# First decoder layer's groups 0 to 5 read as one stream of 64 KiB rows, V's sum kept apart from V, more of the weighting on VectorE

## The chip, the cores and the metric

One NeuronCore of a Trainium2 chip runs the whole kernel. The time is device microseconds of one execution, the median of several runs. VectorE, ScalarE, TensorE and GpSimd are written DVE, ACT, PE and POOL in the profile; SP issues every transfer from device memory.

## What is computed

Two layers of attention, each followed by a small MLP, for one token:

```python
x = x + _A_ref(_layernorm(x), K, V, wq, wo)   # 32 heads, 4096 cached positions, 128 per head
x = x + _B_ref(_layernorm(x), w1, b1, w2, b2) # 512 -> 1376 -> 512, gelu
x = x + _A_ref(_layernorm(x), K, V, wq, wo)   # the same caches and weights again
x = x + _B_ref(_layernorm(x), w1, b1, w2, b2)

def _A_ref(x, k, v, wq, wo):
    q = heads(x @ wq)
    p = softmax(q . k * 128 ** -0.5)          # over the 4096 positions
    return merge(p . v) @ wo
```

Everything is float32. The caches are 64 MiB each and are read once in each layer, so the work is mostly the reading: about 285 MB in all.

## The kernel before

**Groups and chunks.** The 32 heads are taken in 8 groups of 4. K of a group is a block of 128 partitions x 16384 floats (64 KiB on each partition, 8 MiB in all), cut into 8 chunks c = 0 to 7 of 2048 floats (1 MiB); V of a group has the same size and the same cut. A group's slice of `wq`, and of `wo`, is as large as one chunk. The first layer takes the groups in order 0 to 7, the second in the order 7 to 0 and starts on what is still in SBUF. Nearly all of SBUF is one tile, `arena`: three blocks of 8 chunks, then a place for the first `wq` (at `HELD`), and a place of two chunks (`PAIR`) for the weights of a group.

**Order of the transfers.** All are issued by SP through `load` (L87), in program order, and land in that order. In the first layer a group n takes three of them: K (L507, in block (2n+1) mod 3), V (L552, in block (2n+2) mod 3), and one of two chunks with this group's `wo` and the next group's `wq` (L582, in `PAIR`). A transfer is issued when what lay in its place has been read for the last time. SP's queue is in order: a waiting issue holds those behind it.

**A group of the first layer, n = 0 to 5.**
1. `scores` (L232): PE multiplies the query by the 8 chunks of K, into the PSUM bank `pS`.
2. `softmax` (L235 to L255): on DVE the maximum (L236) and small steps, on ACT the exponential (L244), on PE four transposes (L246), on DVE the copy of the weights to `pt` (L248) and the reciprocal of their sum.
3. The weighting of V by `pt`: DVE multiplies chunks 0 to 3, one at a time (`weighted`, L274, 128x2048), ACT chunks 4 to 7 in 16 pieces each (`weighted_by_act`, L269).
4. The sum of the 8 chunks, in the place of chunk 0, on DVE: three adds of two chunks at once (`add_pair`, L279, 128x4096), one of chunk 0 and 1 (L589, 128x2048), one fold to half the length (L287).
5. Between them the next query: `queries` weights `wq` on DVE (L213, L215), PE sums over the partitions (L217), DVE takes the diagonal (L221, L223). Only then can `scores` of the next group begin.
6. The rest is late: inside the next group's `scores`, after chunk 4, PE sums the folded V over the partitions (L292); DVE scales it (L297 to L300) and weights `wo` (L326, L328), which ends the use of `PAIR`; PE adds that to the output row (L332). DVE runs these ahead of the next `softmax`.

DVE's and PE's instructions are pinned in the order of the program (`pin`). Group 6 has PE multiply V by the weights (`values`, L262) in place of steps 3 and 4. Group 7 ends the layer: K in two halves, V in parts, then its `wo`, and after it come `w1`, `w2` and the first of the second layer's K.

Of the kernel before, what the change touches and what calls it, by code (L numbers as in the profile page):

```python
# [55 lines left out]
VAR_AT = 1  # L56
PAIRS = (0, 2, 4, 6), ((4, 6, 0, 2), (2, 0, 4, 6))


@with_exitstack  # L60
def decode_layers(ctx: ExitStack, tc: tile.TileContext, k, v, w, w1, w2, out):
    nc = tc.nc
# [30 lines left out]
    def chunk(t, i=0):  # L93
        return t[:, NC * i : NC * (i + 1)].rearrange("p (j n) -> p j n", j=4)
# [58 lines left out]
    mx, mb = small("mx", 32), small("mb", 32)  # L153
    for t in (zq, mx, mb):
        nc.vector.memset(t, 0.0)

# [78 lines left out]
    def softmax(sc, nsc, p, hold):  # L235
        top = nc.vector.tensor_reduce(mx[:, 0:1], pS, axis=AX.X, op=ALU.max)  # L236
# [11 lines left out]
        nc.vector.tensor_copy(pt, pT[:, :, :, :C].rearrange("p b j c -> p j c b"))  # L248
# [22 lines left out]
    def weighted(pt, t, c):  # L271
        own = t.rearrange("p b (j d) -> p b j d", j=J)
        weight = pt[:, :, c, :].rearrange("p j b -> p b j")[:, :, :, None].to_broadcast([P, 4, J, DH])
        nc.vector.tensor_tensor(own, own, weight, op=ALU.mult)  # L274

# [180 lines left out]
    for layer in range(2):  # L456
# [23 lines left out]
        for n, g in enumerate(order):  # L480
            first, final = n == 0, n == G - 1
            pairs = None
            if layer == 0 and n < G - 2:
                pairs = PAIRS[0]
            if layer == 1 and 1 < n < G - 2:
                pairs = PAIRS[1][n % 2]

# [3 lines left out]

            if layer == 1 and n == 0:
                tiles = [(c, here["k", g, c]) for c in range(C)]
# [14 lines left out]
            for c, t in tiles:  # L508
                scores(z, c, t)
                if late is not None and c == 4:  # L510
                    late[0]()
# [18 lines left out]
            elif layer == 1 and n == 1:  # L530
# [27 lines left out]
            if pairs:  # L558
# [4 lines left out]
                for c in pairs[:2]:  # L563
                    for i in (0, 1):
                        weighted(pt, here["v", g, c + i], c + i)
                add_pair(v_home, *pairs[:2])
# [138 lines left out]
```

## Time and profile before

| | |
|---|---|
| time, median of 3 runs | 673.04 us (672.83 to 673.28) |
| the profiled execution | 672.88 us, of which the span 671.0 us, 1.88 us around it |
| mean granted clock of PE | 0.725 of full speed |
| PE, DVE, ACT busy | 46%, 63%, 32% of the span |
| time that the packets of SP's queue took | 99.2% of the span of 16 DMA engines |
| read from device memory | 284.92 MB, 425 GB/s over the span |

Busy shares are means over stages that differ. For each engine a timeline gives start, duration, line and shapes of its instructions, with the idle time before them and what ended it in square brackets. "Clock" is the share of full speed that PE was granted in a stretch.

### The profile page before, as it was taken

Reading aid. Unit: us, or ns where it says so; the run is one execution under the profiler, and the core shown is the slowest. Engines: PE = TensorE matmul, PEld = TensorE weight load, DVE = VectorE, ACT = ScalarE, POOL = GpSimd, SP = SyncE. Lnnn points to the kernel's source line nnn. Section 1 sums busy time; section 2 is a strip of 40 time slices with the busy share of each in tenths; the row PEclk is TensorE's granted clock in tenths of the full one; section 3 lists DMA queues with packets and bytes.
Section 4 is the critical chain, followed back from the end, with each engine's and each line's share of the span. In section 5 each row is a group of like instructions: output and inputs, shape, how many; then the busy total and the mean of one; then the engine's idle time right before and its main releaser. Section 6 shows DMA issues by size and latency. Waiting matters only on the chain.

```text
span 671.0 us, 5941 instructions
## 1 busy us (share of the span) xinstructions
PE 307.4 (46%) x2196; PEld 83.0 (12%) x2196; DVE 424.0 (63%) x520; ACT 215.3 (32%) x697; POOL 5.2 (1%) x26
## 2 busy tenths in 40 slices
PE   1401603406117054166788985604416126065597
PEld 1100100101001011011124311101101001011124
DVE  3059779598797886972322414289697795983513
ACT  0047064190560823802011200083290650910010
POOL 1000000000000000000000000000000000000000
PEclk9965855857658557577699999755757558567799
DMA  9999999999999999999999999999999999999997
GB/s 377 438 438 438 435 438 438 403 461 438 438 430 404 434 438 426 430 435 425 430 416 403 414 438 439 427 430 438 427 438 438 426 434 405 452 438 417 428 414 300
DMA packets 11548, 285.36 MB, mean 425 GB/s; under 512 B 1280, under 2 KB 1408, under 8 KB 3840
## 3 DMA queue, kind: packets, MB, share of 16 engines
q1 hardware_dynamic: 11520, 284.99, 99.2%
q8 instruction: 17, 0.28, 0.2%
q14 instruction: 11, 0.09, 0.0%
HBM read 284.92 MB, written 0.07 MB: 425 GB/s over the span
## 4 chain that ended last, share of the span: by engine, by line
DMA 65%; PE 20%; DVE 11%; another core or an unknown queue 1%; issue 1%; SPq 1%; ACT 0%; DVEq 0%
DMA arena<-in_k 41%; DMA arena<-in_w 13%; DMA arena<-in_v 12%; PE pS L232 11%; DVE arena L328 4%; PE pO L292 3%; PE pO L262 2%; DVE arena L274 1%; DVE arena L215 1%; DVE arena L297 1%; DVE smalls L299 1%; DVE arena L326 1%; PE pO L430 1%; DVE arena L279 1%
## 5 line engine op out<-in xcount | busy, mean ns | idle before, releaser
L269 ACT ACTIVATE arena<-arena,pt 128x128 f32<-128x128 f32 x640 | 188.0, 386 | 42.7 <-DMA arena<-in_v 38.5
L232 PE MATMUL pS<-arena,smalls 128*8 128x512 f32 x1024 | 142.4, 708 | 78.5 <-DMA arena<-in_k 74.3
L279 DVE TENSOR_TENSOR arena<-arena 128x4096 f32<-128x4096 f32 x30 | 132.6, 4420 | 0.3
L217 PE MATMUL pS<-arena,smalls 128*128 128x512 f32 x20 | 20.8, 1141 | 195.0 <-DVE arena L215 195.0
L244 ACT ACTIVATE arena<-pS,smalls 128x512 f32<-128x512 f32 x16 | 12.4, 777 | 300.9 <-DVE smalls L243 300.9
L274 DVE TENSOR_TENSOR arena<-arena,pt 128x2048 f32<-128x2048 f32 x40 | 89.0, 2286 | 29.0 <-DMA arena<-in_v 26.1
L232 PEld LDWEIGHTS pS<-arena,smalls 128*8 128x8 f32 x1024 | 28.5, 100 | 195.5 <-issue 174.6
L236 DVE TENSOR_REDUCE smalls<-pS 128x1 f32<-128x512 f32 x16 | 11.0, 687 | 61.4 <-PE pS L232 61.4
L262 PE MATMUL pO<-arena,pt 128*4 128x512 f32 x368 | 44.8, 632 | 8.7 <-DMA arena<-in_v 7.9
L304 DVE STREAM_TRANSPOSE arena<-pO 128x512 f32<-128x512 f32 x6 | 4.3, 717 | 57.1 <-PE pO L262 57.1
L215 DVE SCALAR_TENSOR_TENSOR arena<-arena,smalls 128x512 f32<-128x512 f32 x45 | 33.8, 752 | 1.6
L328 DVE SCALAR_TENSOR_TENSOR arena<-arena,smalls 128x512 f32<-128x512 f32 x39 | 29.3, 752 | 1.4
L332 PE MATMUL pB<-arena,smalls 128*1 128x512 f32 x26 | 14.4, 637 | 33.3 <-DVE arena L328 33.3
L217 PEld LDWEIGHTS pS<-arena,smalls 128*128 128x128 f32 x20 | 5.0, 310 | 198.2 <-DVE arena L215 198.2
L297 DVE TENSOR_TENSOR arena<-pO,ident 128x512 f32<-128x512 f32 x10 | 6.9, 692 | 31.3 <-PE pO L292 31.3
L246 PE MATMUL pO<-ident,arena 128*128 128x128 f32 x64 | 13.2, 341 | 25.6 <-ACT arena L244 25.2
L589 DVE TENSOR_TENSOR arena<-arena 128x2048 f32<-128x2048 f32 x10 | 22.9, 2291 | 0.3
L292 PE MATMUL pO<-arena,smalls 128*128 128x512 f32 x40 | 19.8, 618 | 0.0
L399 ACT ACTIVATE smalls<-smalls 128x4 f32<-128x4 f32 (+1 forms) x6 | 1.2, 206 | 43.6 <-DVE smalls L392 25.4
L250 DVE STREAM_TRANSPOSE smalls<-smalls 128x32 f32<-128x32 f32 x16 | 3.4, 212 | 17.4 <-ACT arena L244 17.4
L262 PEld LDWEIGHTS pO<-arena,pt 128*4 128x4 f32 x368 | 9.2, 89 | 41.1 <-issue 35.9
L246 PEld LDWEIGHTS pO<-ident,arena 128*128 128x128 f32 x64 | 8.5, 169 | 39.5 <-ACT arena L244 34.1
(119 smaller groups left out, 211.9 us busy)
## 6 DMA issues: line engine op xcount, KB each, us to landing
arena<-in_w SPq DMA_DIRECT2D x13, 2048.0 KB, 11.5
arena<-in_k SPq DMA_DIRECT2D x5, 4096.0 KB, 21.1
arena<-in_v SPq DMA_DIRECT2D x2, 4096.0 KB, 31.6
arena<-in_w SPq DMA_DIRECT2D x6, 1024.0 KB, 30.9
arena<-in_k SPq DMA_DIRECT2D x1, 6144.0 KB, 19.9
arena<-in_v SPq DMA_DIRECT2D x2, 2048.0 KB, 36.1
arena<-in_w SPq DMA_DIRECT2D x7, 512.0 KB, 11.4
arena<-in_v SPq DMA_DIRECT2D x3, 1024.0 KB, 44.7
```

The lines of the kernel that those rows point to most:

```text
L215: pin(nc.vector.scalar_tensor_tensor(t, wt[:, c, :], xc[:, c : c + 1], t, op0=ALU.mult, op1=ALU.add))
L217: pin(nc.tensor.matmul(at, one.to_broadcast([P, P]), t, start=True, stop=True))
L232: pin(nc.tensor.matmul(pS[32 * j : 32 * j + C, :], z[:, j, C - 1 - c : 2 * C - 1 - c], kt[:, j, :], start=(c == 0), stop=(c == C - 1)))
L246: nc.tensor.transpose(pT[:, b].rearrange("p j r -> p (j r)"), p[:, P * b : P * (b + 1)], ident)
L262: nc.tensor.matmul(pO[32 * j : 32 * j + 4, :], pt[:, j, c, :], by_head(vt)[:, j], start=(i == 0), stop=(i == of - 1))
L269: nc.scalar.activation(own, own, AF.Copy, scale=pt[:, j, c, b : b + 1])
L274: nc.vector.tensor_tensor(own, own, weight, op=ALU.mult)
L279: pin(nc.vector.tensor_tensor(a, a, b, op=ALU.add))
L292: pin(nc.tensor.matmul(pO, one.to_broadcast([P, P]), total[:, b, :], start=b == 0, stop=b == n - 1))
L328: pin(nc.vector.scalar_tensor_tensor(t, wt[:, d, :], on[:, d : d + 1], t, op0=ALU.mult, op1=ALU.add))
L332: pin(nc.tensor.matmul(pB[0:1, :], one, t, start=n == 0, stop=n == G - 2))
L589: pin(nc.vector.tensor_tensor(total, total, other, op=ALU.add))
```

## The change

**The stream.** K, V, `wo` and `wq` of groups 0 to 5, and K of group 6, become units of one chunk in the order of use: k0 (8 units), v0 (8), wq1, k1 (8), wo0, v1 (8), wq2, k2 (8), wo1 and so on. The host cuts this list into rows: row 0 has 4 units, rows 1 to 14 have 8 each (64 KiB on each partition). Each row is one transfer into block (r+2) mod 3. Row r is issued when all units of row r-3 are used up (`flow`, `done`), so a row now holds parts of K, V and weights, and waits for the last use of any of them. What the prediction speaks of: row 6 is v2; row 8 is k3 chunk 7, wo2 and v3 chunks 0 to 5; row 9 takes row 6's place, row 11 takes row 8's.

**V's sum.** It gets a place of its own behind the three blocks (`total`), no longer that of V's chunk 0.

**The weighting.** `weighted_two` multiplies two neighbouring chunks at once (128x4096). A table gives each group the chunks that ACT weights and the order of the steps on DVE: `W` two chunks multiplied, `w` one, `a24` chunks 4, 5 added to 2, 3, `s01` the first two into the sum, `t2` one more into the sum, `q` the next query's weighting, `r` its diagonal. `LATE` says after which chunk of the next `scores` the late sum is put. ACT weights 12 of 48 chunks, before 24; DVE weights 36.

**Softmax, both layers.** The reciprocal is taken of the 32-wide broadcast, in place of a copy and a reciprocal of one column; one instruction fewer. In the second layer the pairs that DVE weights are also taken two at once.

The core of the diff (all of the table but two lines, and the host's packing, left out):

```diff
+PLANS = (
...
+    ((5, 6, 7), "W01 W23 a02 w4 a04 a06 q s01 r"),
+    ((2, 3, 6), "W01 W45 s01 a24 w7 t2 q t3 r t6 t7"),
...
+LATE = 6, 6, 4, 4, 6, 6
...
-        lt, l, lr, rl = small("mt", 32), small("l"), small("lr", 32), small("rl")
+        lt, l, lr = small("mt", 32), small("l"), small("lr", 32)
         nc.vector.transpose(lt, mx)
         nc.vector.tensor_reduce(l, lt[:, :C], axis=AX.X, op=ALU.add)
-        nc.vector.tensor_copy(lt, l.to_broadcast([P, 32]))
+        nc.vector.reciprocal(lt, l.to_broadcast([P, 32]))
         nc.vector.transpose(lr, lt)
-        nc.vector.reciprocal(rl, lr[:, 0:1])
-        return pt, rl
+        return pt, lr[:, 0:1]
...
+    def weighted_two(pt, t, c):
+        own = t.rearrange("p (b j d) -> p b j d", j=J, d=DH)
+        weight = pt[:, :, c : c + 2, :].rearrange("p j c b -> p (c b) j")[:, :, :, None].to_broadcast([P, 8, J, DH])
+        return nc.vector.tensor_tensor(own, own, weight, op=ALU.mult)
...
+    def early_values(n, pt, xc):
+
+        by_act, plan = PLANS[n]
+        total = chunk(arena[:, 3 * BLOCK : 3 * BLOCK + NC])
+        for c in by_act:
+            weighted_by_act(pt, here["v", n, c], c)
+        steps = plan.split()
...
+        a, b = steps.index("q"), steps.index("r")
+        for s in steps[:a]:
+            step(s)
+        z = queries(n + 1, xc, here["wq", n + 1, 0], pS, short=True,
+                    between=lambda: [step(s) for s in steps[a + 1 : b]])
+        done(("wq", n + 1, 0))
+        for s in steps[b + 1 :]:
+            step(s)
+        return z, total, folded(total)
...
+    def flow():
+
+        while len(loaded) < len(ROWS) and (len(loaded) < 3 or used.issuperset(ROWS[len(loaded) - 3])):
+            r = len(loaded)
+            loaded.append(load((r + 2) % 3 * BLOCK, rows_of[r][:, : NC * len(ROWS[r])]))
...
+    def done(*units):
+        used.update(units)
+        flow()
...
             for c, t in tiles:
                 scores(z, c, t)
-                if late is not None and c == 4:
+                if layer == 0 and n <= EARLY:
+                    done(("k", n, c))
+                if late is not None and c == (4 if layer else LATE[n - 1]):
                     late[0]()
...
+            elif early:
+                z, total, n_left = early_values(n, pt, xc_l)
+
+                def late_sum(rl=rl, ot=ot, n=n, total=total, n_left=n_left):
+                    sum_of_folded(total, n_left)
+                    summed_wo(scaled_out_of_folded(rl, ot), here["wo", n, 0], ot[:, :U])
+                    done(("wo", n, 0))
```

**SP at the start of the program, before:** `in_w` brings the weights, `in_k` and `in_v` the caches; a size is partitions x floats.

```order
L87 DMA arena<-in_w 128x2112
L87 DMA arena<-in_k 128x16384
L87 DMA arena<-in_v 128x16384
L87 DMA arena<-in_w 128x4096
L87 DMA arena<-in_k 128x16384
L87 DMA arena<-in_v 128x16384
```

The same place now, `in_rows` being the new array:

```order
L105 DMA arena<-in_w 128x2112
L105 DMA arena<-in_rows 128x8192
L105 DMA arena<-in_rows 128x16384 x14
L105 DMA arena<-in_v 128x16384
L105 DMA arena<-in_w 128x4096
```

Nineteen transfers (seven of K, six of V, six of weights) became fifteen; after them comes V of group 6 as before.

**DVE in group 2, from the weighting of V to the fold, before** (`arena<-arena,pt` is a multiplication by the weights, `arena<-arena` an addition, `pS` the next query's sum):

```order
L274 TENSOR_TENSOR arena<-arena,pt 128x2048 x4
L279 TENSOR_TENSOR arena<-arena 128x4096
L213 TENSOR_SCALAR arena<-arena,smalls 128x512
L215 SCALAR_TENSOR_TENSOR arena<-arena,smalls 128x512 x3
L279 TENSOR_TENSOR arena<-arena 128x4096
L221 TENSOR_TENSOR arena<-pS,ident 128x512
L223 TENSOR_REDUCE smalls<-arena 128x4
L279 TENSOR_TENSOR arena<-arena 128x4096
L589 TENSOR_TENSOR arena<-arena 128x2048
L287 TENSOR_TENSOR arena<-arena 128x1024
```

The same stretch of group 2 now:

```order
L296 TENSOR_TENSOR arena<-arena,pt 128x4096 x2
L322 TENSOR_TENSOR arena<-arena 128x4096
L291 TENSOR_TENSOR arena<-arena,pt 128x2048
L322 TENSOR_TENSOR arena<-arena 128x4096 x2
L231 TENSOR_SCALAR arena<-arena,smalls 128x512
L233 SCALAR_TENSOR_TENSOR arena<-arena,smalls 128x512 x3
L327 TENSOR_TENSOR arena<-arena 128x2048
L239 TENSOR_TENSOR arena<-pS,ident 128x512
L241 TENSOR_REDUCE smalls<-arena 128x4
L351 TENSOR_TENSOR arena<-arena 128x1024
```

One more chunk is multiplied, and the next query's steps (L231 to L241) moved from the middle of the additions to their end.

**DVE in group 3 now** (before, group 3 had the same rows as group 2):

```order
L296 TENSOR_TENSOR arena<-arena,pt 128x4096 x2
L327 TENSOR_TENSOR arena<-arena 128x2048
L322 TENSOR_TENSOR arena<-arena 128x4096
L291 TENSOR_TENSOR arena<-arena,pt 128x2048
L327 TENSOR_TENSOR arena<-arena 128x2048
L231 TENSOR_SCALAR arena<-arena,smalls 128x512
L233 SCALAR_TENSOR_TENSOR arena<-arena,smalls 128x512 x3
L327 TENSOR_TENSOR arena<-arena 128x2048
L239 TENSOR_TENSOR arena<-pS,ident 128x512
L241 TENSOR_REDUCE smalls<-arena 128x4
L327 TENSOR_TENSOR arena<-arena 128x2048 x2
L351 TENSOR_TENSOR arena<-arena 128x1024
```

Five chunks are weighted on DVE where it was four, single additions take the place of double ones, and the third L327 (step `t3`), which row 11 waits for, stands behind the next query's weighting (L231, L233).

More of the change, by code (lines that the diff above doesn't have):

```diff
@@ L153, in decode_layers @@
     mx, mb = small("mx", 32), small("mb", 32)
-    for t in (zq, mx, mb):
-        nc.vector.memset(t, 0.0)
+    for t, start in ((zq, 0.0), (mx, 1.0), (mb, 0.0)):
+        nc.vector.memset(t, start)
     def of_32(t, n, i=0):
@@ L273, in weighted, with two, step @@
         weight = pt[:, :, c, :].rearrange("p j b -> p b j")[:, :, :, None].to_broadcast([P, 4, J, DH])
-        nc.vector.tensor_tensor(own, own, weight, op=ALU.mult)
+        return nc.vector.tensor_tensor(own, own, weight, op=ALU.mult)
+    def weighted_two(pt, t, c):
+        own = t.rearrange("p (b j d) -> p b j d", j=J, d=DH)
+        weight = pt[:, :, c : c + 2, :].rearrange("p j c b -> p (c b) j")[:, :, :, None].to_broadcast([P, 8, J, DH])
+        return nc.vector.tensor_tensor(own, own, weight, op=ALU.mult)
+    def two(n, c):
+        row = next(r for r in range(len(ROWS)) if ("v", n, c) in ROWS[r])
+        i = ROWS[row].index(("v", n, c))
+        assert ROWS[row][i + 1] == ("v", n, c + 1)
+        return loaded[row][:, NC * i : NC * (i + 2)]
+    def early_values(n, pt, xc):
[4 more added lines that the diff above has]
+        steps = plan.split()
+        def step(s):
+            c = int(s[1])
+            if s[0] == "w":
+                pin(weighted(pt, here["v", n, c], c))
+                return
+            if s[0] == "W":
+                pin(weighted_two(pt, two(n, c), c))
+                return
+            if s[0] == "a":
+                by = int(s[2])
+                pin(nc.vector.tensor_tensor(two(n, c), two(n, c), two(n, by), op=ALU.add))
+                done(("v", n, by), ("v", n, by + 1))
+                return
+            first = here["v", n, c] if s[0] == "s" else total
+            c = int(s[-1])
+            pin(nc.vector.tensor_tensor(total, first, here["v", n, c], op=ALU.add))
+            done(*(("v", n, int(i)) for i in s[1:]))
+        a, b = steps.index("q"), steps.index("r")
[7 more added lines that the diff above has]
+        return z, total, folded(total)
     def add_pair(at, to, by):
@@ L482, in decode_layers @@
             pairs = None
-            if layer == 0 and n < G - 2:
-                pairs = PAIRS[0]
             if layer == 1 and 1 < n < G - 2:
-                pairs = PAIRS[1][n % 2]
+                pairs = PAIRS[n % 2]
+            early = layer == 0 and n < EARLY
             k_home, v_home = ((2 * n + i) % 3 * BLOCK for i in (1, 2))
@@ L490, in decode_layers @@
                 k_home, v_home = K2_HOME if n == 2 else 15 * NC, 6 * NC * (n % 2)
-            if layer == 1 and n == 0:
+            if layer == 0 and n <= EARLY:
+                flow()
+                tiles = ((c, here["k", g, c]) for c in range(C))
+            elif layer == 1 and n == 0:
                 tiles = [(c, here["k", g, c]) for c in range(C)]
@@ L509, in decode_layers @@
                 scores(z, c, t)
-                if late is not None and c == 4:
+                if layer == 0 and n <= EARLY:
+                    done(("k", n, c))
+                if late is not None and c == (4 if layer else LATE[n - 1]):
                     late[0]()
@@ L563, in decode_layers @@
                 for c in pairs[:2]:
-                    for i in (0, 1):
-                        weighted(pt, here["v", g, c + i], c + i)
+                    weighted_two(pt, arena[:, v_home + NC * c : v_home + NC * (c + 2)], c)
                 add_pair(v_home, *pairs[:2])
```

28 lines of the change are left out of this document (26 added, 2 removed), and 4 rows, old and new, of the table PLANS.

## The prediction

> **What bounds the kernel now.** I read the page first: is there anything but the reading of memory?
>
> ```profile
> GB/s 377 438 438 438 435 438 438 403 461 438 438 430 404 434 438 426 430 435 425 430 416 403 414 438 439 427 430 438 427 438 438 426 434 405 452 438 417 428 414 300
> ...
> q1 hardware_dynamic: 11520, 284.99, 99.2%
> HBM read 284.92 MB, written 0.07 MB: 425 GB/s over the span
> ```
>
> The transfer engines are taken 99.2% of the span. So a change gains only by making the bytes come faster, and loses as soon as SP issues a row too late. The question is whether the new rows come free in time. PE's timeline gives the pace, since a burst of scores begins when K has landed:
>
> ```profile
> 24.88 8.39 PE L232 MATMUL pS<-arena,smalls 128*8 128x512 f32 x64 [12.55 <-DMA arena<-in_k]
> 113.75 5.75 PE L232 MATMUL pS<-arena,smalls 128*8 128x512 f32 x40 [6.04 <-DMA arena<-in_k]
> 119.43 1.98 PE L292 MATMUL pO<-arena,smalls 128*128 128x512 f32 x4
> 149.31 2.07 PE L217 MATMUL pS<-arena,smalls 128*128 128x512 f32 x2 [20.05 <-DVE arena L215]
> 157.43 6.09 PE L232 MATMUL pS<-arena,smalls 128*8 128x512 f32 x40 [6.04 <-DMA arena<-in_k]
> 288.45 7.13 PE L232 MATMUL pS<-arena,smalls 128*8 128x512 f32 x40 [6.04 <-DMA arena<-in_k]
> ```
>
> A group, 18 chunks of 1 MiB, takes 157.43 - 113.75 = 43.68 us, 2.427 us a chunk; four groups to 288.45 give the same. That is 18.87 MB in 43.68 us, 432 GB/s.
>
> DVE's timeline shows how much room a group leaves (groups 0, 1 and 2; the number in front is the start):
>
> ```profile
> 33.34 0.69 DVE L236 TENSOR_REDUCE smalls<-pS 128x1 f32<-128x512 f32 x1 [19.91 <-PE pS L232]
> 38.26 0.27 DVE L248 COPY pt<-pO 128x128 f32<-128x128 f32 x1
> ...
> 121.45 0.69 DVE L297 TENSOR_TENSOR arena<-pO,ident 128x512 f32<-128x512 f32 x1 [2.30 <-PE pO L292]
> ...
> 125.93 0.68 DVE L236 TENSOR_REDUCE smalls<-pS 128x1 f32<-128x512 f32 x1
> ...
> 129.39 0.25 DVE L248 COPY pt<-pO 128x128 f32<-128x128 f32 x1
> ...
> 133.14 8.90 DVE L274 TENSOR_TENSOR arena<-arena,pt 128x2048 f32<-128x2048 f32 x4 [3.44 <-DMA arena<-in_v]
> ...
> 146.42 0.48 DVE L213 TENSOR_SCALAR arena<-arena,smalls 128x512 f32<-128x512 f32 x1
> ...
> 149.18 4.42 DVE L279 TENSOR_TENSOR arena<-arena 128x4096 f32<-128x4096 f32 x1
> 153.51 0.69 DVE L221 TENSOR_TENSOR arena<-pS,ident 128x512 f32<-128x512 f32 x1
> ...
> 154.83 4.42 DVE L279 TENSOR_TENSOR arena<-arena 128x4096 f32<-128x4096 f32 x1
> ...
> 161.61 1.22 DVE L287 TENSOR_TENSOR arena<-arena 128x1024 f32<-128x1024 f32 x1
> ```
>
> Weighting to fold runs from 133.14 to 162.83: 29.7 us. Sum on PE and its wait: 121.45 - 119.43 = 2.0. From there to the next maximum: 125.93 - 121.45 = 4.5. Softmax to the end of the copy of the weights: 129.64 - 125.93 = 3.7. Together 39.9 of 43.7 us; the rest is waiting for K and V (the 3.44 us in brackets). DVE has under 4 us to give per group.
>
> **The change part by part.** *The rows.* Seven K, six V and six weight transfers become fifteen. Nothing shows a gap between transfers: most slices of the page move 438 GB/s against the 432 of a group, and if merging brought all of it to 438, a group would take 43.1 us, 3.6 us less over six groups. The lower end is nothing, since the bytes are the same. I take 0.4 us, near the lower end, because the three transfers of a group are already issued together and queue up behind each other; a loss has no mechanism here as long as rows are issued in time.
>
> *VectorE and ScalarE.* Prices:
>
> ```profile
> L279 DVE TENSOR_TENSOR arena<-arena 128x4096 f32<-128x4096 f32 x30 | 132.6, 4420 | 0.3
> L274 DVE TENSOR_TENSOR arena<-arena,pt 128x2048 f32<-128x2048 f32 x40 | 89.0, 2286 | 29.0 <-DMA arena<-in_v 26.1
> ```
> ```profile
> 133.13 18.80 ACT L269 ACTIVATE arena<-arena,pt 128x128 f32<-128x128 f32 x64 [4.58 <-DMA arena<-in_v]
> ```
>
> A two-chunk multiplication isn't in the trace. Its bounds are the addition of that size, 4.42 us, and two single ones, 8.90 / 2 = 4.45; I take 4.42. One-chunk steps cost 2.29, the next query 2.76 + 1.32 (146.42 to 149.18, 153.51 to 154.83), the fold 1.22. The old group had five one-chunk and three two-chunk steps: 5 x 2.29 + 3 x 4.42 + 4.08 + 1.22 = 30.0 against 29.7 measured, so I take 0.3 off each sum (steps overlap a little). Weighting to fold now, by the order of the steps (number of two-chunk steps, of one-chunk steps, and the sum in us):
>
> - group 0: 6, 3: 38.4
> - group 1: 5, 4: 36.3
> - group 2: 5, 2: 31.7
> - group 3: 3, 6: 32.0
> - group 4: 5, 3, and 0.7 us until ACT's two chunks (18.80 / 2 = 9.4 us beside two double steps of 8.8): 34.7
> - group 5: 4, 4: 31.8
>
> All six exceed the old 29.7, and with 2.0 + 4.5 + 3.7 = 10.2 us after the fold none fits into 43.7 by much: DVE becomes a chain without pauses, and its lateness adds up. ACT's pieces run beside these steps and, but for those 0.7 us, end before they are needed; without that cover a chunk would cost 4.7 us. The second layer's pairs taken two at once save 0.3 us a group in front of a wait for V (the 26.1 us behind L274): nothing. Softmax loses one small step (0.15 us) and takes a reciprocal over 32 columns that no row shows: between the 0.15 of one column and the 0.69 of a pass over 512; I take no net change.
>
> *PE's clock.* The groups of five chunks of scores above take 5.75 to 7.13 us from a standstill, because they start slowly:
>
> ```profile
> 114.00:116.00 2.00, 2.00 (x12) 0.33 (x8) 1.97 (x2) 0.00 (x0) 0.00 (x0) 0.50 0.45 197
> 118.00:120.00 2.00, 2.00 (x18) 0.55 (x11) 1.15 (x1) 0.00 (x0) 0.00 (x0) 1.00 1.21 524
> 130.00:148.00 18.00, 0.00 (x0) 0.00 (x0) 14.75 (x8) 14.87 (x51) 0.00 (x0) 0.50 1.05 452
> ```
>
> The third number from the end is the granted clock: half speed after idle time, full after some 3 us of work. Before, the sum always followed a burst at full clock, two products in 1.98 us. At half clock one product took 2.07 (the L217 row). Now PE has multiplied the first seven chunks (6.3 + 2 x 0.9 us after the query) some 6 to 9 us before the fold in groups 2 and 6, and idles; two products then take about 3.6 us: 1.6 more, bounded by 0 (PE still warm) and 2.1 (two at 2.07). The Trainium skill, "TensorE: Matmul & The Clock Gate", Part 1, says that a gap of more than about 3.4 us halves the clock; by that rule both sums are slow, and the trace agrees (0.50 from 130 to 148 us, without a product).
>
> *The chain.* Row 1 holds k0's second half and lands at 24.88 + 4 x 2.427 = 34.6. Four cold chunks, about 5.4 (of 8.39 for eight), then the first softmax, 33.34 to 38.53 = 5.2: weighting starts at W0 = 45.2. Then fold F0 = 83.6, W1 = 93.8, F1 = 130.1; cold sum, W2 = 130.1 + 11.8 = 141.9. In group 2 the next query ends at 141.9 + 31.7 - 1.2 = 172.4, later than row 7's and 8's landing, so five cold chunks (6.3) come behind it, then 2.0 + 4.5 + 3.7: W3 = 188.9. In group 3 step `t3` ends after 3 double, 4 single steps and 2.76, less 0.3, 24.9 us: 213.8. That frees row 8 for row 11.
>
> *The deadline.* Row 5 ends after as many bytes as k2 before, at 113.7; each later row 8 x 2.427 = 19.4 us on: row 8 at 171.9, row 10 at 210.7. The smallest transfer shows the lead that an issue needs:
>
> ```profile
> out<-arena SPq DMA_DIRECT2D x1, 64.0 KB, 1.5
> ```
>
> It takes 1.5 us from issue to landing, so row 11 must be issued by 209.2. It is 4.6 us late (with no lead at all, 3.1), and the transfer engines stand still. Row 9, freed at W2 + 29.1 = 171.0, is due at 170.4: about 0.6 late, inside the 4.6. Behind row 11 in SP's queue stand rows 12 to 14 and group 6's V; by the same sums their places come free 4 us or more before the shifted landings ask for them, so they add nothing.
>
> *The end of the layer.* In group 3 the next query ends at W3 + 26.2 = 215.1; then 6.3 + 10.2: W4 = 231.6, F4 = 266.3, W5 = 276.5, F5 = 308.3, cold sum, and group 6's weights are ready at 320.1. Before, group 6 waited for V:
>
> ```profile
> 307.82 8.56 PE L262 MATMUL pO<-arena,pt 128*4 128x512 f32 x64 [2.01 <-DMA arena<-in_v]
> ...
> 341.89 3.62 PE L262 MATMUL pO<-arena,pt 128*4 128x512 f32 x32 [1.33 <-DMA arena<-in_v]
> ...
> 354.26 1.05 PE L344 MATMUL pS<-arena,smalls 128*1 128x128 f32 x32 [0.28 <-DMA arena<-in_w]
> ```
> ```profile
> 339.72 0.25 DVE L248 COPY pt<-pO 128x128 f32<-128x128 f32 x1
> 350.39 0.72 DVE L304 STREAM_TRANSPOSE arena<-pO 128x512 f32<-128x512 f32 x1 [10.36 <-PE pO L262]
> 353.16 0.22 DVE L321 SCALAR_TENSOR_TENSOR smalls<-pt,smalls 128x4 f32<-128x4 f32 x1
> ```
>
> From 307.82 to group 7's weights is 32.15 us, so these come at 352.3. From there L304 comes after 350.39 - 341.89 = 8.5 and L321 ends after 3.0 more, of which I take 0.6 as waits for V that are gone: L344 at 363.2, 8.9 later than 354.26. There loads of 0.5 MB queue in front of the second layer:
>
> ```profile
> arena<-in_k SPq DMA_DIRECT2D x3, 512.0 KB, 5.8
> ```
>
> Of 5.8 us, 1.5 is the lead and 1.2 the transfer (0.52 MB at 432 GB/s): 3.1 us of queue absorbs part, 5.8 remains. The row's 4.6 lies inside it, for both count the same lost transfer time. What follows is bound by transfers and keeps the loss; the last stage isn't touched. The 0.4 of the rows falls before the standstill and only lengthens it.
>
> So 672.88 + 5.8 = 678.7 for a profiled execution; the median lies 0.16 above it: **678.8 us**.
>
> **The rivals.** *All rows in time* (0.10): the chain is 4.6 us shorter up to row 11 and 5.8 up to the second layer. For it: three times cold scores and two cold sums are worth up to 9 us if PE stays at full clock, and an issue may need less lead. Against: idle PE shows 0.50 above. Time: 673.04 - 0.4 = 672.6, no change; it decides if `t3` ends before 209.2.
>
> *The rows win* (0.08): as above, and transfers run at the best slice's rate: up to 3.6 us less, 670 to 671.5. A rule has the same sign: the Trainium skill, "DMA: Bandwidth & Descriptors", Anatomy of one DMA, gives every transfer a fixed 2 us beside its bytes at 436 GB/s; by it four fewer would save an estimated 8 us, 665, and a group of three would take 43.3 + 6.0 = 49.3. The measured 43.68 speaks against it: that cost is hidden here.
>
> *DVE's lateness isn't absorbed at all* (0.07): no queue at the layer's end, scores at the slow end of 5.75 to 7.13, the reciprocal at 0.5: 8.9 + 3 x 0.8 + 6 x 0.35 = 13 us, 686.
>
> **How the numbers follow.** My forecast has 0.75. Its own range: scores 5.75 to 7.13 three times (-1.7, +2.5), the cold sums (-3.2, +1.0), the lead and the queue (1.5 either way), not all at once: 674.5 to 682.5. Holding eight in ten takes in the in-time case: 672.4 to 683. A measurement can tell about 0.2%, 1.35 us, from no change. Faster 0.08; within it 0.10; slower the rest, 0.82.
>
> **What would show it.** Right: DVE almost without idle time between weighting and fold from 45 to 320 us, W1 to W5 near 94, 142, 189, 232, 277; SP's row 11 issued near 214 behind DVE; a dip in GB/s there; group 6's products near 320. Wrong: row 11 issued before 209, group 6's products still waiting for V, sums at full clock in groups 2 and 6, or a group's landing under 43.1 us.

## The result and the profile after

The changed kernel takes 688.12 us (median of six runs, 687.09 to 689.62), the one before 673.03 beside it (672.82 to 673.41): a ratio of 1.0225, with a 95% interval of 1.0212 to 1.0238. That is 15.1 us slower where 5.8 was forecast; the sign is right, the size well under half. The profiled execution took 689.62 us, with a span of 687.8, 16.8 us longer than the span before; it is the slowest of the six, so its rows show some 1.5 us more loss than the median. Traces are compared below by their spans, kernels by their ratios to the kernel before.

The page of the changed kernel: its transfers, and the shares of the chain of waits that ended last:

```profile
GB/s 425 431 427 427 424 431 427 428 427 366 366 454 333 431 427 427 431 428 433 426 415 298 331 444 418 455 431 427 415 442 443 431 435 418 448 427 416 431 415 286
...
q1 hardware_dynamic: 10944, 284.99, 97.2%
...
DVE 43%; DMA 32%; PE 20%; ACT 2%; issue 2%; SPq 0%; ACTq 0%; DVEq 0%
```

The shares of the chain in the kernel before:

```profile
DMA 65%; PE 20%; DVE 11%; another core or an unknown queue 1%; issue 1%; SPq 1%; ACT 0%; DVEq 0%
```

DVE has taken the place of the transfers in the chain. The queue was taken 99.2% of the span before and is at 97.2% now, and three places in the row of GB/s are low that were not: slices 10 and 11 (366, 366), 13 (333), and 22 and 23 (298, 331). The same places by stretches, with two more for PE's clock (busy time and count of PE, PE's loads, DVE, ACT, POOL; then granted clock, transfers' share, GB/s):

```profile
150.00:170.00 20.00, 0.00 (x0) 0.00 (x0) 19.65 (x9) 7.61 (x27) 0.00 (x0) 0.50 0.97 420
170.00:176.00 6.00, 3.72 (x10) 0.78 (x14) 5.40 (x5) 0.00 (x0) 0.00 (x0) 0.50 0.52 175
...
214.00:220.00 6.00, 4.50 (x18) 0.83 (x22) 5.93 (x5) 0.00 (x0) 0.00 (x0) 0.50 0.56 197
...
268.00:270.00 2.00, 0.04 (x1) 0.04 (x1) 1.87 (x2) 0.00 (x0) 0.00 (x0) 1.00 1.21 524
270.00:272.00 2.00, 2.00 (x3) 0.93 (x4) 0.00 (x0) 0.00 (x0) 0.00 (x0) 0.59 1.13 492
...
375.00:379.00 4.00, 3.83 (x76) 1.86 (x69) 0.63 (x3) 0.21 (x1) 0.74 (x2) 1.00 0.27 53
```

From 170 to 176 us and from 214 to 220 the transfers move 175 and 197 GB/s, less than half of the 420 from 150 to 170, while DVE is busy nearly all the time; from 375 to 379, between the layers, they move 53 GB/s while PE is busy. Which transfers are missing? SP's timeline and, of the same four issues (rows 8 to 11), the time from issue to landing:

```profile
139.47 0.33 SPq L105 DMA_DIRECT2D arena<-in_rows  x1
...
172.98 0.33 SPq L105 DMA_DIRECT2D arena<-in_rows  x1
...
184.51 0.33 SPq L105 DMA_DIRECT2D arena<-in_rows  x1
...
216.11 0.33 SPq L105 DMA_DIRECT2D arena<-in_rows  x1
```
```profile
arena<-in_rows SPq DMA_DIRECT2D x1, 32.2
...
arena<-in_rows SPq DMA_DIRECT2D x1, 22.4
...
arena<-in_rows SPq DMA_DIRECT2D x1, 30.3
...
arena<-in_rows SPq DMA_DIRECT2D x1, 23.3
```

Row 8 lands at 139.47 + 32.2 = 171.7; row 9 is issued only at 172.98, into an empty queue, and lands at 195.4, 23.7 us behind row 8 instead of 19.4. Row 10 lands at 214.8, row 11 is issued at 216.11 and lands at 239.4, 24.6 us behind. Rows 9 and 11 are the two whose deadline the prediction had worked out. DVE's timeline shows what they waited for (the starts of the weighting in groups 2, 3 and 5, the steps `s01` and `t3` that use up rows 6 and 8, the folds, and a copy of the softmax):

```profile
143.48 8.76 DVE L296 TENSOR_TENSOR arena<-arena,pt 128x4096 f32<-128x4096 f32 x2
...
170.63 2.28 DVE L327 TENSOR_TENSOR arena<-arena 128x2048 f32<-128x2048 f32 x1
...
174.22 1.22 DVE L351 TENSOR_TENSOR arena<-arena 128x1024 f32<-128x1024 f32 x1
...
190.97 0.29 DVE L266 COPY pt<-pO 128x128 f32<-128x128 f32 x1 [0.38 <-PE pO L264]
...
191.31 8.75 DVE L296 TENSOR_TENSOR arena<-arena,pt 128x4096 f32<-128x4096 f32 x2
...
213.68 2.28 DVE L327 TENSOR_TENSOR arena<-arena 128x2048 f32<-128x2048 f32 x1
...
221.90 1.23 DVE L351 TENSOR_TENSOR arena<-arena 128x1024 f32<-128x1024 f32 x1
...
282.07 4.42 DVE L296 TENSOR_TENSOR arena<-arena,pt 128x4096 f32<-128x4096 f32 x1
```

`s01` ends at 172.91 and row 9 goes out 0.07 us later; `t3` ends at 215.96, row 11 goes out 0.15 us later. PE's timeline tells what stands between DVE's steps and how the layer ends:

```profile
44.10 0.63 PE L264 MATMUL pO<-ident,arena 128*128 128x128 f32 x4 [4.12 <-ACT arena L262]
...
131.03 3.78 PE L356 MATMUL pO<-arena,smalls 128*128 128x512 f32 x4 [9.47 <-DVE arena L351]
...
142.00 1.12 PE L264 MATMUL pO<-ident,arena 128*128 128x128 f32 x4 [1.52 <-ACT arena L262]
...
174.36 6.35 PE L250 MATMUL pS<-arena,smalls 128*8 128x512 f32 x40 [1.51 <-DVE smalls L241]
...
217.40 7.02 PE L250 MATMUL pS<-arena,smalls 128*8 128x512 f32 x40 [1.50 <-DVE smalls L241]
...
269.96 3.44 PE L356 MATMUL pO<-arena,smalls 128*128 128x512 f32 x4 [2.19 <-DVE arena L351]
...
314.32 3.78 PE L356 MATMUL pO<-arena,smalls 128*128 128x512 f32 x4 [6.16 <-DVE arena L351]
...
326.80 9.50 PE L279 MATMUL pO<-arena,pt 128*4 128x512 f32 x64 [0.38 <-DVE pt L266]
...
371.12 0.39 PE L408 MATMUL pS<-arena,smalls 128*1 128x128 f32 x6
```

Group 6's products wait for DVE's copy, no longer for V, and begin 19.0 us later than before (326.80 against 307.82). L408, the L344 of the kernel before, begins at 371.12 against 354.26: 16.9 us, as much as this execution lost in all (16.8). After it the queue runs empty; the next load into it, 0.52 MB issued at 377.13 us, takes this long to land:

```profile
arena<-in_w SPq DMA_DIRECT2D x1, 512.0 KB, 3.7
```

### The profile page after: what moved, and what is told of

Read it like the earlier page. It is cut to its first block, busy times and chain, and to the rows that moved or that the text cites. A ratio compares the mean times of both kernels' runs of the same rounds, so it can differ in the third digit from the quotient of the medians.

```text
span 687.8 us, 5719 instructions
## 1 busy us (share of the span) xinstructions
PE 327.5 (48%) x2196; PEld 85.9 (12%) x2196; DVE 450.9 (66%) x498; ACT 159.1 (23%) x505; POOL 5.2 (1%) x26
## 3 DMA queue, kind: packets, MB, share of 16 engines
q1 hardware_dynamic: 10944, 284.99, 97.2%
## 4 chain that ended last, share of the span: by engine, by line
DVE 43%; DMA 32%; PE 20%; ACT 2%; issue 2%; SPq 0%; ACTq 0%; DVEq 0%
DMA arena<-in_v 26%; DVE arena L296 14%; DVE arena L322 8%; PE pS L250 6%; PE pO L279 6%; DVE arena L327 5%; DMA arena<-in_rows 5%; DVE arena L343 3%; PE pO L356 2%; DVE arena L233 2%; DVE arena L392 2%; DMA arena<-in_w 2%; ACT arena L286 1%; DVE arena L291 1%; PE pO L264 1%
## 5 line engine op out<-in xcount | busy, mean ns | idle before, releaser
L250 PE MATMUL pS<-arena,smalls 128*8 128x512 f32 x1024 | 150.4, 741 | 59.9 <-DMA arena<-in_k 24.7
L286 ACT ACTIVATE arena<-arena,pt 128x128 f32<-128x128 f32 x448 | 131.9, 388 | 21.5 <-DMA arena<-in_v 13.8
L296 DVE TENSOR_TENSOR arena<-arena,pt 128x4096 f32<-128x4096 f32 x24 | 105.5, 4421 | 8.5 <-DMA arena<-in_v 8.3
L322 DVE TENSOR_TENSOR arena<-arena 128x4096 f32<-128x4096 f32 x12 | 53.1, 4422 | 1.1 <-ACT arena L286 0.6
L343 DVE TENSOR_TENSOR arena<-arena 128x4096 f32<-128x4096 f32 x12 | 53.0, 4420 | 0.1
L279 PE MATMUL pO<-arena,pt 128*4 128x512 f32 x368 | 51.1, 669 | 3.8 <-DMA arena<-in_v 2.7
L327 DVE TENSOR_TENSOR arena<-arena 128x2048 f32<-128x2048 f32 x18 | 41.2, 2290 | 0.4
L396 PE MATMUL pB<-arena,smalls 128*1 128x512 f32 x26 | 18.3, 796 | 39.0 <-DVE arena L392 39.0
L233 DVE SCALAR_TENSOR_TENSOR arena<-arena,smalls 128x512 f32<-128x512 f32 x45 | 33.8, 752 | 1.6
L356 PE MATMUL pO<-arena,smalls 128*128 128x512 f32 x40 | 24.9, 754 | 19.1 <-DVE arena L351 19.1
L264 PE MATMUL pO<-ident,arena 128*128 128x128 f32 x64 | 14.6, 369 | 23.0 <-ACT arena L262 22.7
L279 PEld LDWEIGHTS pO<-arena,pt 128*4 128x4 f32 x368 | 10.1, 92 | 38.2 <-issue 35.1
## 6 DMA issues: line engine op xcount, KB each, us to landing
arena<-in_w SPq DMA_DIRECT2D x7, 2048.0 KB, 11.5
```

Of the source, the lines that this page charges most:

```text
L233: pin(nc.vector.scalar_tensor_tensor(t, wt[:, c, :], xc[:, c : c + 1], t, op0=ALU.mult, op1=ALU.add))
L250: pin(nc.tensor.matmul(pS[32 * j : 32 * j + C, :], z[:, j, C - 1 - c : 2 * C - 1 - c], kt[:, j, :], start=(c == 0), stop=(c == C - 1)))
L279: nc.tensor.matmul(pO[32 * j : 32 * j + 4, :], pt[:, j, c, :], by_head(vt)[:, j], start=(i == 0), stop=(i == of - 1))
L286: nc.scalar.activation(own, own, AF.Copy, scale=pt[:, j, c, b : b + 1])
L296: return nc.vector.tensor_tensor(own, own, weight, op=ALU.mult)
L322: pin(nc.vector.tensor_tensor(two(n, c), two(n, c), two(n, by), op=ALU.add))
```

## Experiments

The theory that was tested: DVE's chain of steps, with PE at half clock inside it, uses up rows too late and then ends the layer late. Against it: the mixed rows cost time by themselves, or long rows are read faster and something else is slow.

**ScalarE with 21 of the 48 chunks, and an order that uses rows up early** (12 chunks in the changed kernel, 24 before):

```diff
 PLANS = (
-    ((), "W01 W23 a02 s01 W45 q W67 r a46 t4 t5"),
-    ((7,), "W01 s01 W23 q W45 r w6 a24 a26 t2 t3"),
...
+    ((0, 1, 6, 7), "W23 W45 a02 s01 t7 t5 q t6 r t4"),
+    ((2, 6, 7), "w3 W01 a20 W45 s67 q t5 r t4 t3 t2"),
+    ((2, 3, 4, 5), "W01 W67 a06 s23 q t0 t5 r t1 t4"),
+    ((2, 3, 6, 7), "W45 W01 a04 q a02 r s01 t7 t6"),
+    ((0, 4, 5), "W23 w1 a02 s01 q W67 r a46 t4 t5"),
+    ((5, 6, 7), "W01 w4 W23 q a20 r a24 a26 s23"),
 )
-LATE = 6, 6, 4, 4, 6, 6
+LATE = 4, 4, 4, 4, 4, 5
```

> The stream of rows and V's own place for the sum stay as in the changed kernel; only the table is another: ScalarE weights 4, 3, 4, 4, 3, 3 chunks of groups 0 to 5 (21 of 48, not 12), and the order of DVE's steps is chosen so that rows are used up early. All work is done. Theory C (DVE's chain of steps, lengthened by PE at half clock, frees rows 9 and 11 too late and then ends the layer late): adding up the changed kernel's own durations, every row is issued at least 2.9 us before the row ahead of it has landed, group 6's weights are ready near 309 us (326.8 in the changed kernel), no standstill, and the time is the old one, 672 to 674 us. Rival R (mixed rows, one transfer that waits for the last use of eight chunks of three kinds, cost time by themselves): still 680 us or more, with standstills. Rival G (long rows are read faster once they are in time): under 671 us.

Measured: 673.28 us, a ratio to the kernel before of 0.9994 (0.9985 to 1.0003). Its page, and PE at the end of the layer:

```profile
GB/s 377 437 437 438 434 438 437 434 433 434 437 437 434 426 418 426 434 434 426 427 412 399 412 436 428 434 438 437 423 441 433 430 434 404 464 437 401 430 416 291
```
```profile
307.76 8.68 PE L279 MATMUL pO<-arena,pt 128*4 128x512 f32 x64 [1.18 <-DMA arena<-in_v]
...
354.20 1.05 PE L408 MATMUL pS<-arena,smalls 128*1 128x128 f32 x32 [0.29 <-DMA arena<-in_w]
```

No slice of the first layer is low; group 6's products wait for V again and begin within 0.06 us of where they did. All 15.1 us come back without touching the rows, V's sum, the softmax or the second layer's pairs: together these cost nothing that can be measured, and bring nothing either. (A small gain of one that another takes away is not excluded.) This run changes DVE's amount of work and the order of its steps at once; the next two take them apart.

**DVE's share as small as before and its steps in the old order**, on the new rows (the same line for all six groups):

```diff
 PLANS = (
-    ((), "W01 W23 a02 s01 W45 q W67 r a46 t4 t5"),
...
+    ((4, 5, 6, 7), "W01 W23 a02 q a04 r a06 s01"),
...
-LATE = 6, 6, 4, 4, 6, 6
+LATE = 4, 4, 4, 4, 4, 4
```

> The new rows and V's own place for the sum, but in groups 0 to 5 ScalarE weights chunks 4 to 7 and DVE's steps stand in the order of the kernel before (two chunks multiplied at once, three additions of two chunks, chunks 0 and 1 summed last). DVE's work is as small as before; all work is done. If the rows' deadlines decide, not the amount of DVE's work: V's first chunk is used up last and holds its row, so that rows 4, 6, 13 and 15 are 8 to 10 us late each; adding up the durations, 705 to 712 us. If the amount on DVE decides and the rows set no deadline of their own: 672.5 to 675.

Measured: 712.17 us, ratio 1.0568 (1.0551 to 1.0585), 0.2 us above the range foreseen. The page, and the products of group 6, which wait 11 us for V:

```profile
GB/s 415 413 420 465 189 458 299 333 431 417 442 435 366 461 421 214 436 296 336 407 434 413 398 409 439 428 413 454 431 439 425 426 445 425 436 431 418 428 418 292
```
```profile
345.92 9.27 PE L279 MATMUL pO<-arena,pt 128*4 128x512 f32 x64 [10.99 <-DMA arena<-in_v]
```

Slices 5, 7 and 8, 16, 18 and 19 are the standstills at rows 4, 6 and 13 and at group 6's V. So the rows do set deadlines of their own, and DVE's amount of work alone doesn't decide: chunk 0 of V, summed last, holds the whole row in which it lies. They cost nothing only if the table of steps meets the deadlines.

**The changed kernel's shares, another order.** ScalarE keeps 0, 1, 3, 3, 2 and 3 chunks:

```diff
-    ((5, 6, 7), "W01 W23 a02 w4 a04 a06 q s01 r"),
-    ((2, 3, 6), "W01 W45 s01 a24 w7 t2 q t3 r t6 t7"),
+    ((4, 5, 7), "W01 W23 w6 a24 q a06 r s01 t2 t3"),
+    ((1, 6, 7), "w0 W45 W23 a24 q a20 r s23 t6 t7"),
...
-LATE = 6, 6, 4, 4, 6, 6
+LATE = 4, 5, 6, 5, 6, 4
```

> The changed kernel's shares, ScalarE 0, 1, 3, 3, 2, 3 chunks of groups 0 to 5, so DVE has exactly as much to do; but which chunks, and the order of the steps, are chosen anew so that rows come free earlier. All work is done. If order and amount both count: by adding up durations, some 3.3 us are lost at row 6, 2.2 at row 9, 1.3 at row 13, none at row 11; group 6's weights near 317 to 320; 679 to 683 us, about half of the changed kernel's loss. If only the amount on DVE counts: 687 to 689. If only the order counts: 673 to 675.

Measured: 680.14 us, ratio 1.0113 (1.0090 to 1.0136), group 6's products at 319.37:

```profile
319.37 9.30 PE L279 MATMUL pO<-arena,pt 128*4 128x512 f32 x64 [0.38 <-DVE pt L266]
```

The profiled execution, at 683.37 us, is the slowest of its four. Which chunks DVE takes, and in what order, gives back half (1.0225 to 1.0113, 7.5 us) with the amount of work unchanged. The other half came back only in the run that also takes work from DVE; that no order alone could do it is not shown.

**The old transfers, six chunks on DVE.** The kernel before, groups 0 to 5:

```diff
-                for c in pairs[2:]:
+                by_act = pairs[2:] if layer else pairs[3:]
+                for c in by_act:
                     for i in (0, 1):
                         weighted_by_act(pt, here["v", g, c + i], c + i)
                 for c in pairs[:2]:
+                    if layer == 0:
+                        weighted_two(pt, arena[:, v_home + NC * c : v_home + NC * (c + 2)], c)
+                        continue
                     for i in (0, 1):
                         weighted(pt, here["v", g, c + i], c + i)
                 add_pair(v_home, *pairs[:2])
+                if layer == 0:
+                    c = pairs[2]
+                    weighted_two(pt, arena[:, v_home + NC * c : v_home + NC * (c + 2)], c)
```

> The kernel before, with its old transfers, sum and softmax; of groups 0 to 5, DVE weights six chunks (three multiplications of two chunks), ScalarE two. All work is done. Theory C: weighting to fold grows by 4.2 us, 29.7 to about 33.9, a group on DVE to about 44.1 plus 1 for slow sums, against 43.7; the lateness adds up to some 6 to 10 us at group 6 (its products near 315 to 318 in place of 307.8), no standstill before, since K and V come free as blocks long ahead; the end of the layer costs the larger part of it: 677 to 682 us. Rival R (it was the rows): no change, 672.5 to 674.

Measured: 679.36 us, ratio 1.0078 (1.0065 to 1.0092), 5.3 us. The time is within what was expected, the way to it is not. SP's first and last issue of a group's two chunks of weights, five groups apart, and PE:

```profile
85.04 0.33 SPq L87 DMA_DIRECT2D arena<-in_w  x1
...
308.46 0.33 SPq L87 DMA_DIRECT2D arena<-in_w  x1
```
```profile
312.50 8.95 PE L262 MATMUL pO<-arena,pt 128*4 128x512 f32 x64 [0.38 <-DVE pt L248]
```

These two land 10.2 and 10.1 us after their issue, so 223.3 us apart; in the kernel before, the same two were issued at 81.69 and 302.17 and landed 12.6 and 10.4 us later, 218.3 us apart. The weights' place `PAIR` comes free with the weighting of `wo` on DVE, K and V stand behind them in SP's queue, and so DVE's lateness reaches the transfers: five groups cost 5.0 of the 7.3 us by which this execution is longer. It is not spread evenly: three of the five rounds still take 43.6 to 43.9 us from landing to landing, two take 46.0 and 46.2. The products of group 6 are late by 4.7, no more; the expectation that the end of the layer costs the larger part, and that nothing stands still before it, was wrong.

**The end of the layer by itself.** The changed kernel with one multiplication of two chunks left out in group 4 and one in group 5:

```diff
-    ((2, 3), "W01 W45 a02 s01 q W67 r a46 t4 t5"),
-    ((5, 6, 7), "W01 s01 W23 q w4 r a24 a26 t2 t3"),
+    ((2, 3), "W01 a02 s01 q W67 r a46 t4 t5"),
+    ((5, 6, 7), "W01 s01 q w4 r a24 a26 t2 t3"),
```

> The changed kernel, but one multiplication of two chunks is left out in group 4 (chunks 4 and 5) and one in group 5 (chunks 2 and 3), so that V goes unweighted there; groups 0 to 3 are as they were. If the late end of the layer is a loss of its own beside the standstills at rows 9 and 11 (theory C): both standstills stay (3.6 us each), group 6's products begin near 318 in place of 326.8, the standstill of 5.4 us between the layers goes, and the time is 680 to 683 us, 5 to 8 less than the changed kernel. If the end of the layer takes up lateness and only the rows count: 687 to 689, no change. If all the loss comes from the end of the layer: 673 to 675.

Measured: 684.28 us, ratio 1.0153 (1.0139 to 1.0167), 4.8 us less than the changed kernel and 1.3 us above the range foreseen. Its page and PE:

```profile
GB/s 386 457 449 430 427 427 430 373 430 430 346 438 319 435 430 430 430 427 411 436 414 412 383 428 420 460 434 430 402 459 434 430 427 412 449 434 418 436 411 283
```
```profile
323.53 8.42 PE L279 MATMUL pO<-arena,pt 128*4 128x512 f32 x64 [0.38 <-DVE pt L266]
```
```profile
245.72 4.42 DVE L322 TENSOR_TENSOR arena<-arena 128x4096 f32<-128x4096 f32 x1 [5.06 <-ACT arena L286]
```

The standstills of the rows stay (346, 319, and here also 373 at row 7, which was not foreseen), the slices between the layers, 22 and 23, read 412 and 383 instead of 298 and 331. Row 11 is issued at 217.19 us and lands 23.7 later, at 240.9; in the run with 21 chunks on ScalarE it landed at 229.8, 11.1 us earlier, and that execution was 11.5 us shorter (671.3 and 682.8). So nearly all that is left is the rows' loss. The loss at the end of the layer is one of its own, and the 3.3 us by which group 6 comes earlier were enough to end it. They are fewer than the two multiplications (8.8 us) because DVE waits 5.1 us for ScalarE's chunks in group 4, the last line.

**PE kept warm.** Three tries, with idle products between the real ones. The first:

```diff
+        for _ in range(5):
+            idle(before, pK[0])
...
+            for _ in range(13 if steps[a + 1][0] == "W" else 7):
+                idle(warm_t, pK[0])
...
+                        for _ in range((6, 30, 0, 0, 8, 30)[n - 1]):
+                            idle(warm_t, pK[0])
```

> The changed kernel with idle products of 8 columns for PE, into a PSUM bank that is not used yet: five before the next query's sum, 7 or 13 behind it, up to 30 before the sum of the folded V, 6 before the transposes of the softmax, in groups 0 to 5. The work itself is unchanged. Theory C with PE's clock as the decisive addition: with scores at 0.87 us a chunk from the first, sums at 2.0 and transposes at 0.66, the chain adds up to group 6's weights near 315 to 318, row 9 about 0.2 us late and row 11 about 2, and the time comes to 676 to 680 us. If the clock matters little: 686 to 689, and if the idle products only come in the way: over 690.

Measured: 802.91 us, ratio 1.188. The idle products came in the way:

```profile
73.83 10.90 PE L544 MATMUL pK<-arena,ident 128*8 128x512 f32 x25
```

A float32 product stands as two records (five idle products as ten), so these are 12 to 13 products of 0.87 us, although the four products of 8 rows for a chunk of scores take 0.9 together (4.48 us for five chunks, in the third try). That had been overlooked: the idle products were reckoned at a quarter of their time. The second try made them a quarter as long, `idle(warm_t, pK[0], P)`:

> As the kernel with idle products before, but each idle product takes 128 columns in place of 512, since one of 512 took 0.87 us at full clock and 1.3 us when cold there (four of 8 rows in four places of a bank take no longer than one), four times what had been reckoned; a small one should take about 0.2 to 0.33. The work itself is unchanged. If PE's clock is the decisive addition to DVE's chain: group 6's weights near 316 to 320 in place of 326.8, row 9 some 0.5 us and row 11 some 2.5 us short, 676 to 680 us. If the clock matters little: 686 to 689.

Measured: 697.64 us, ratio 1.0348 (1.0320 to 1.0375), and spoiled by its own waits: the products read `PAIR`, so group 6's weights, and all behind them in SP's queue, waited for the last of them (SP 36.7 us in one wait), and those ahead of the transposes held the softmax up. What it still shows, in stretches around its last sum:

```profile
313.00:314.00 1.00, 0.33 (x4) 0.04 (x1) 1.00 (x1) 0.00 (x0) 0.00 (x0) 1.00 0.61 262
...
315.00:316.00 1.00, 0.62 (x2) 0.39 (x3) 0.32 (x1) 0.00 (x0) 0.00 (x0) 0.99 0.61 262
316.00:317.00 1.00, 1.00 (x3) 0.48 (x2) 0.00 (x0) 0.00 (x0) 0.00 (x0) 0.50 0.46 197
```

The clock falls to half at 316, behind a pause of only some 2 us. The third try:

```diff
-    warm_t = arena[:, PAIR : PAIR + U].rearrange("p (j n) -> p j n", j=1)
+    warm_t = arena[:, HELD + 2 * NC + 1100 : HELD + 2 * NC + 1100 + P].rearrange("p (j n) -> p j n", j=1)
...
-                if layer == 0:
-                    for _ in range(6):
-                        idle(warm_t, pK[0], P)
...
-                        for _ in range((6, 30, 0, 0, 8, 30)[n - 1]):
+                        for _ in range((6, 47, 0, 0, 8, 38)[n - 1]):
```

> The changed kernel with small idle products (8 rows by 128 columns, 0.22 us at full clock) for PE in groups 0 to 5, now free of the two waits that spoiled the earlier tries: they read a place of their own that no transfer needs, and none stands before the softmax's transposes. Five go before the next query's sum, 7 or 13 behind it, 6, 47, 0, 0, 8, 38 before the sums of the folded V. The work itself is unchanged. If PE's half clock lengthens DVE's chain: scores of groups 3 and 4 in 4.5 us in place of 6.35 and 7.02, the sums of groups 2, 5 and 6 in 2.0 in place of 3.79, 3.45 and 3.79; together 9.4 us, so that group 6's weights are ready near 317 to 319, row 11 is issued 3 to 4 us earlier, the standstills at rows 9 and 11 shrink from 9.6 to about 5.5 us in all, the loss between the layers nearly goes, and the time is 678 to 682 us. If the clock isn't on the path: 687 to 690.

Measured: 683.86 us, ratio 1.0161 (1.0140 to 1.0182), 4.3 us less than the changed kernel. Sums of groups 1 and 6, scores of group 4, products of group 6 (the sum's line, L356 before, is L366 here):

```profile
84.20 1.98 PE L366 MATMUL pO<-arena,smalls 128*128 128x512 f32 x4 [2.76 <-DVE arena L361]
...
215.44 4.48 PE L250 MATMUL pS<-arena,smalls 128*8 128x512 f32 x40 [0.33 <-DVE smalls L241]
...
310.06 1.98 PE L366 MATMUL pO<-arena,smalls 128*128 128x512 f32 x4
...
320.74 9.38 PE L279 MATMUL pO<-arena,pt 128*4 128x512 f32 x64 [0.38 <-DVE pt L266]
```

The sums and the scores of group 4 have full clock. Not all has: from 173 to 176 us, as the scores of group 3 begin, PE's mean clock is 0.62, and most transposes still take 1.1 us. The chain is 6.1 us shorter at group 6, where 9.4 had been reckoned, and row 11 goes out only 2.0 us earlier (214.12), so the time is 2 us above the range. The clock is on the path: this run gives back 4.3 us, somewhat under a third of the loss.

**One late row, with DVE in time.** The kernel with 21 chunks on ScalarE reads a column of row 6 once more, so that row 9 goes out late: ahead of the weighting of `wo` in one kernel, behind it in the other.

```diff
     def done(*units):
-        used.update(units)
+        used.update(u for u in units if u != ("v", 2, 4))
         flow()
...
+    def read_late(n):
+        if n == 2:
+            pin(nc.vector.tensor_copy(small("seen"), here["v", 2, 4][:, 0, 0:1]))
+            used.add(("v", 2, 4))
+            flow()
```

> The kernel in which ScalarE weights 21 chunks and all rows are in time (673.3 us), with one thing added: DVE reads one column of row 6 once more, behind the scaling of group 2's output in group 3, so that row 9 can be issued only near 170.9 us, 0.3 us before row 8 has landed. DVE's chain has 2 to 3 us to spare there. All work is done. If a row must be issued about 3 us before the row ahead of it has landed (the changed kernel's 19.6, 23.8 and 24.5 us from landing to landing at -2.5, +1.6 and +1.7): the interval from row 8's landing to row 9's is near 22 in place of 19.4, and the time is 675.5 to 676.5. With the 1.5 us of the prediction: 1.2 us lost, 674.5. If a single late row is made good later: 673.3.

Measured: 677.87 us, ratio 1.0056 (1.0041 to 1.0071). Row 9's issue (row 10's follows 0.4 us behind, so SP shows two), and row 9's time to landing:

```profile
171.41 0.81 SPq L105 DMA_DIRECT2D arena<-in_rows  x2
```
```profile
arena<-in_rows SPq DMA_DIRECT2D x1, 22.3
```

> As the kernel with row 9 issued just before row 8 has landed, but the extra reading stands behind the weighting of wo, so that row 9 is issued near 174.6, 3.4 us after row 8 has landed. All work is done. With a lead of about 3 us: the interval from landing to landing near 25.7, 6.3 us lost, 679 to 680.5 us. With 1.5 us of lead: 4.9 lost, 678.2. If made good later: 673 to 675.

Measured: 680.91 us, ratio 1.0105 (1.0088 to 1.0122):

```profile
174.70 0.80 SPq L105 DMA_DIRECT2D arena<-in_rows  x2
```
```profile
arena<-in_rows SPq DMA_DIRECT2D x1, 22.3
```

Both rows land 22.3 us after their issue, where the bytes take 19.4: an empty queue costs 2.9 us, about the 3 expected and twice the 1.5 of the prediction. Issued 3.3 us later, the second lands 3.3 later, and the time is 3.0 us longer: nothing of it is made good. Against the kernel with all rows in time, where row 9 landed at 191.0, it lands 2.7 and 6.0 us later, and the time grows by 4.2 and 7.5 us (by the ratios; 0.4 to 1.4 us more than expected). The 1.5 us beyond row 9 in both are open.

## Why the prediction was right in sign and too small

- **What bounds the kernel; little room on DVE.** Right. The kernel with 21 chunks on ScalarE shows that what hides under the transfers costs nothing, and the other kernels that steps beyond it cost time.
- **The rows: 0.4 us.** Right that they bring next to nothing: with every row in time the ratio is 0.9994, and most slices of the first layer read 434 to 438, as before. "The rows win" falls with that run.
- **VectorE's sums.** Right. A multiplication of two chunks takes 4.42 us (8.76 for two). Group 2 from W to the end of the fold: 143.48 to 175.44, 32.0 us (forecast 31.7); group 3: 191.31 to 223.13, 31.8 (32.0). Over all six groups the sums were 1.0 us too short.
- **Softmax: no net change.** Right while PE's transposes are slow: DVE's copy of the weights waits 0.38 us for them (the row at 190.97), and the wider reciprocal, 0.35 us, lies ahead of it. In groups 1, 2, 5 and 6 its path ends only 0.1 us ahead of the transposes, so behind fast transposes it could show.
- **PE's clock and the chain.** The step that failed first. "Two products then take about 3.6 us" in groups 2 and 6 was right (3.78), but of all that stands between fold and weighting, the prediction let half clock lengthen only those two sums and the scores. Group 5's sum took 3.44 us where 2.0 was put in. The transposes took 1.12 us in most groups, where group 0's took 0.63, and the 3.7 us of softmax had been read behind a burst at full clock; it is 4.1 in groups 1 to 6. The scores of group 4 took 7.02 in place of 6.3. These add up to 4.6 us by group 6. Forecast and measured start of the weighting: group 2 141.9 and 143.5, group 3 188.9 and 191.3, group 5 276.5 and 282.1; group 6's weights 320.1 and 326.8. Of these last 6.7 us, 1.0 are in VectorE's sums, 5.6 between fold and weighting.
- **The deadline.** The second step that failed: "It takes 1.5 us from issue to landing" is the lead of one transfer of 64 KB out of the chip, not that of a row into an empty queue, which here takes 22.3 to 23.3 us for 19.4 us of bytes: 2.9 to 3.9 us. Why row 11 took 0.9 us more than row 9 is open. Row 11 landed at 239.4, where 210.7 + 19.4 = 230.1 was possible: 9.3 us lost through it instead of 4.6. Of the difference, 2.3 is the later chain (issue at 216.11, not 213.8) and 2.4 the lead (3.9, not 1.5). That row 9 lies inside row 11's lateness was right as a sum: it lost 4.3 us of the 9.3 first.
- **The end of the layer.** Here the rest is missing. L408 came at 371.12, not 363.2: 7.9 us, of which 6.7 is the lateness of group 6's weights and most of the rest slower products (9.50 in place of 8.56 at 326.80). And "3.1 us of queue absorbs part" rested on the same 1.5. The load that is issued into an empty queue at 377.13 us takes 3.7 us for its 1.2 us of bytes, a lead of 2.5. That leaves 2.1 us of queue, and 16.9 less 2.1 is 14.8 us, against 16.8 measured; the forecast was 8.9 less 3.1. So of the 11.0 us that this execution lost beyond the forecast, 7.9 are the later chain and 1.0 the longer lead. Some 2 us are open: the first scores of the second layer begin 15.4 us later than before (386.31 and 370.94), but the loads around them come slowly (225 to 334 GB/s from 384 to 388 us), and the last 4 MB of their K lands 16.8 us later (408.4 and 391.6). The run with groups 4 and 5 lightened shows this loss apart from the rows'.
- **The rivals.** "DVE's lateness isn't absorbed at all", 686 us, was nearest: in the end nothing was absorbed, and its 13 us were still 2 too few. That it came so near is partly luck: it took the scores at their slowest and a reciprocal of 0.5 us (measured: 0.35), not the sums, the transposes or the lead. "All rows in time" needed `t3` before 209.2; it ended at 215.96.
- **The range.** It gave the lead "1.5 either way" and the cold work a few terms, but let neither pull twice, although both move row 11 and the layer's end in the same direction. Even with all its upper ends at once (2.5, 1.0 and 1.5 us) it would have ended at 683.8.

Of the clock, the Trainium skill, "TensorE: Matmul & The Clock Gate", Part 1, says that it halves after an idle window of about 3.4 us, and that the windows run freely. The prediction read this as a gap of more than 3.4 us. The runs differ: group 5's sum came after a gap of 2.19 us, at full clock for its first moments and then 0.59 (the rows from 268 to 272); so did the sum behind 2 us in the second try, while a gap of 2.76 in the third left it at 1.98 us. By these runs a gap of 2 us can already be too long, and one of 2.76 us need not be, so the length of the gap alone doesn't decide. Windows that run freely would explain it, which no run here tested.

## What to carry to other kernels

Where transfers run without pause, a resource that is reused sets a deadline for the engine that frees it: add up the engine's chain to each deadline, with half-clock prices for every product that may stand behind a pause, and ask for a lead as long as a transfer into an empty queue costs, not a small one's latency. Larger, mixed transfers move the deadlines without moving the bytes, so the order of the steps must be chosen anew with them: here the same multiplications and additions cost 0, 15 or 38 us by their order and by their share between the engines alone. Lateness costs time at every stage that has no slack, and how much slack a stage has is read from how early its transfers are issued.

## Not expected of the hardware

- A row of 8 MiB into an empty queue takes 22.3 to 23.3 us from issue to landing in the four cases shown, and 21.8 to 23.1 in four more, in the two runs with other orders; in a filled queue a row lands 19.4 us behind the one ahead.
- Four products of 8 rows and 512 columns into four parts of a PSUM bank take 0.9 us together, one alone 0.87.
- The clock fell behind pauses of 2.05 and 2.19 us and held through 2.76.
- One trap of reading, of the profile and not of the chip: the chain of waits of the changed kernel shows "issue" from 200.12 to 202.18, which looks like DVE waiting for ScalarE's chunk. DVE's own timeline has an addition of 2.29 us there: a pause in the chain is a pause only if the engine's timeline has it too.
